# Gated products of x with [w1 | w2] from seven block products instead of eight

## The chip, the cores and the metric

The kernel runs on one core of a Trainium2 chip. TensorE (PE) multiplies matrices into eight PSUM banks; VectorE (DVE), ScalarE (ACT) and GpSimd (POOL) work on SBUF, and the first two also read PSUM; SyncE (SP) and other queues issue DMAs. The metric is device time in microseconds, of which lower is better.

## The reference, cut to what matters

```python
# attention without softmax: 2 batches x 8 heads, 576 tokens, head_dim 64 -> x (1152 tokens x 512)
def _moe_ref(x, w1, w2, w3, w_out):     # w1, w2: 512 x 1024, w3: 1024 x 1024, w_out: 1024 x 512
    a = x @ w1
    b = x @ w2
    h = a * b @ w3
    return (h @ w_out).astype(np.float32)

def _moe2_ref(x, domain_probs, w1, w2): # 4 experts, w1[e]: 512 x 1024, w2[e]: 1024 x 512
    p = domain_probs / (domain_probs.sum(-1, keepdims=True) + 1e-09)
    for e in range(E):
        h = np.maximum(x @ w1[e], 0.0)
        out += p[:, e:e + 1] * (h @ w2[e])
```

The weights arrive as 64-bit floats and everything is computed in 32 bits.

## The kernel before, in words

**Numbers on PE.** Each 32-bit operand is held as two tiles side by side, a high part that PE multiplies exactly (`HI`) and the remainder (`LO`). A product takes three matmuls (`PASSES`: low by high, high by low, high by high). `split` (L81, L82) makes the two: ACT copies the high part, DVE (or POOL, where `eng` says so) subtracts it from the source. `from_f64` turns a DMA'd tile of 64-bit floats into a 32-bit tile, with one instruction on ACT (L97) and two on DVE (L98, L99).

**Stages on PE, in order.** (1) Attention for eight `Pair`s of heads (four pairs for each of two batches), whose steps are transposes of q and k, exponential features with a running maximum (`mx`, L326), sums, attended values and `place`, which puts a pair's result as a 128-row block of x transposed into `xt`. Pair n's steps run beside pair n-1's. The last 64 tokens of each batch (the tail) are done by `attend_tail`, four pairs at once. (2) The fold of w3 and w_out into one 1024 x 512 matrix `w3o` (`fold`, L207), which fills PE beside the attention. (3) The gated units: unit `b02` is batch 0, columns 256 to 383 of w1 and w2. A unit takes 48 matmuls (2 weights x 4 blocks of d_model x 3 passes x 2 halves of the tokens) of 128 x 288 (L165) into four banks; ACT copies the two halves of a (L172), DVE multiplies those of b onto them (L176) and the result is split into `hid`. There are 16 units. (4) `expert_input` (`c0`, `c1`, L226): hid by w3o, per batch, 192 matmuls each. (5) Four experts, each in two halves of its columns, with products of seven block products already (L721, L803).

**What sets the order.** `BESIDE` lists what is issued beside each pair (o: load a block of w_out; f: fold; w: load a block of w1 and w2; b: gated unit), `AFTER` what follows the last. A scheduler interleaves ready work from the neighbouring steps, by priority; after that each engine runs its own instructions strictly in that order, and a waiting instruction holds up all behind it. `load_w12(g)` prepares w1's and w2's columns of unit number g (two tiles of 128 x 512, high parts by ACT, low parts by POOL).

**Memory.** Tiles come from pools on the left or right side of SBUF; `mctx` closes after c1 and what it held is used again by the experts. `raw_p` takes the expert weights as they come from memory.

Of the kernel before, what the change touches and what calls it, by code (L numbers as in the profile page):

```python
# [45 lines left out]
def attention_moe_kernel(ctx: ExitStack, tc: tile.TileContext, q, k, v, omega, mw1, mw2, mw3, mwo, probs, ew1, ew2, out):  # L46
# [108 lines left out]
    def gated(a_p, bufs, b, g, tags):  # L155

        pool = xt_p if len(hid) < XT_BUFS - 2 * KD else h_p
        ht = hid[b, g] = pool.tile([P, 2, S], F32R, tag=pool.name, name="hid")
        halves = []
        for w in range(2):  # L160
            bs = [bank(tags[2 * w + c]) for c in range(2)]
            for kk in range(KD):
                for n, (x, y) in enumerate(PASSES):
                    for c in range(2):
                        nc.tensor.matmul(  # L165
                            out=bs[c][:, :HS], lhsT=w12[w, g][:, x, kk], rhs=xt[b][kk][:, y, c * HS:(c + 1) * HS],
                            start=(kk == 0 and n == 0), stop=(kk == KD - 1 and n == 2),
                        )
            for c in range(2):
                if w == 0:  # L170
                    t = a_p.tile([P, HS], F32, tag="a", name="a", bufs=bufs)
                    nc.scalar.activation(out=t, in_=bs[c][:, :HS], func=ACTF.Copy)  # L172
                    halves.append(t)
                else:
                    t, s = halves[c], slice(c * HS, (c + 1) * HS)
                    nc.vector.tensor_tensor(out=t, in0=bs[c][:, :HS], in1=t, op=ALU.mult)  # L176
                    split(ht[:, HI, s], ht[:, LO, s], t)
# [88 lines left out]
    with ExitStack() as actx:  # L266
# [624 lines left out]
```

## Time and profile before

| | |
|---|---|
| median of three runs | 669.43 us (669.23 to 673.52) |
| profiled execution, first to last instruction | 669.8 us |
| busy: PE, DVE, ACT, POOL | 655.5, 465.9, 414.2, 122.2 us |
| first gated matmul to first matmul of c0 | 132.75 to 248.62 us |
| granted TensorE clock, mean | 0.997 of full speed |

The profiled execution has no other time of its own than its span, which lies 0.4 us above the median. Busy time of an engine is no bound by itself: what counts is the stretch in which it is the one that others wait for.

### The profile page before, as it was taken

The page shows a single profiled execution, that of the slowest core. Times are in us where ns is not written, and L with a number is a line of the kernel's source. Part 1 is how long each engine was busy: PE and PEld are TensorE (multiplying, and loading weights), DVE is VectorE, ACT ScalarE, POOL GpSimd, SP SyncE. Part 2 cuts the span into 40 slices and gives each one's busy share as a digit, 9 for nine tenths or more (in the row PEclk, how much of TensorE's full clock was granted, in tenths as well). Part 3 has the DMA queues.
Part 4 walks back from the last instruction along what each step waited for, and adds up shares of the span by engine and source line. Part 5 has one row for each costly group of instructions (what it writes and reads, how often), then busy time and mean ns, then how long its engine had stood idle before and what let it go on. Part 6 is the DMA issues. An engine that isn't in the chain of part 4 may idle for free.

```text
span 669.8 us, 12373 instructions
## 1 busy us (share of the span) xinstructions
PE 655.5 (98%) x4831; PEld 628.4 (94%) x4831; DVE 465.9 (70%) x770; ACT 414.2 (62%) x895; POOL 122.2 (18%) x145
## 2 busy tenths in 40 slices
PE   8999999999999999999999999999999999999997
PEld 5888888899999999999899999999999998999996
DVE  3859977776572234357959867868689588687795
ACT  3997637583552233347768768778587777687740
POOL 2331000131240000000022241321331313304200
PEclk8999999999999999999999999999999999999999
DMA  9859443345110001002245484681882855837725
GB/s 222 280 180 201 123 115 95 126 133 183 45 52 1 1 1 64 1 1 83 76 132 138 56 144 101 110 154 38 158 142 35 148 117 90 142 71 103 121 60 173
DMA packets 58091, 70.59 MB, mean 105 GB/s; under 512 B 8817, under 2 KB 43121, under 8 KB 58033
## 3 DMA queue, kind: packets, MB, share of 16 engines
q1 hardware_dynamic: 44704, 49.05, 25.4%
q0 software_dynamic: 12640, 20.19, 20.5%
q8 instruction: 38, 0.62, 0.4%
q10 hardware_dynamic: 688, 0.56, 0.3%
q14 instruction: 21, 0.16, 0.1%
HBM read 47.24 MB, written 22.54 MB: 104 GB/s over the span
## 4 chain that ended last, share of the span: by engine, by line
PE 80%; DVE 6%; DMA 5%; issue 4%; ACT 4%; SPq 1%; POOL 1%; DVEq 0%; ACTq 0%; POOLq 0%
PE ps_f L721 6%; PE ps_f L803 6%; PE ps_po L207 3%; PE ps_x L721 3%; PE ps_w L721 3%; PE ps_et L721 3%; PE ps_kv L721 3%; PE ps_t L721 3%; PE ps_po L721 3%; PE ps_x L803 3%; PE ps_et L803 3%; PE ps_t L803 3%; PE ps_kv L803 3%; PE ps_w L207 3%; PE ps_f L165 3%
## 5 line engine op out<-in xcount | busy, mean ns | idle before, releaser
L755 POOL DMA_DIRECT2D out_dram<-o x98 | 81.6, 892 | 356.5 <-DVE o L780 174.9
L82 DVE TENSOR_TENSOR hs<-hd,hs 128x1024 fp32r<-128x1024 f32 x48 | 58.2, 1216 | 1.5 <-ACT hs L81 1.5
L81 ACT ACTIVATE hs<-hd 128x1024 fp32r<-128x1024 f32 x48 | 50.6, 1055 | 5.7 <-DVE hd L617 4.6
L705 ACT ACTIVATE hd<-hd 128x288 f32<-128x288 f32 x96 | 40.7, 438 | 9.0 <-DVE hd L703 8.5
L721 PE MATMUL ps_f<-x,w1e 128*128 128x288 f32 x288 | 46.2, 294 | 0.0
L617 DVE TENSOR_TENSOR hd<-hd 128x512 f32<-128x512 f32 x64 | 43.8, 684 | 0.8
L617 DVE TENSOR_TENSOR raw<-raw 128x512 f32<-128x512 f32 x64 | 43.8, 685 | 0.5
L803 PE MATMUL ps_f<-w2e,hs 128*128 128x256 f32 x288 | 43.2, 282 | 0.0
L82 DVE TENSOR_TENSOR w2e<-raw,w2e 128x1024 fp32r<-128x1024 f32 x32 | 38.8, 1217 | 5.4 <-ACT w2e L81 5.3
L721 PEld LDWEIGHTS ps_f<-x,w1e 128*128 128x128 f32 x288 | 40.9, 188 | 0.1
L803 PEld LDWEIGHTS ps_f<-w2e,hs 128*128 128x128 f32 x288 | 38.5, 191 | 0.1
L81 ACT ACTIVATE w2e<-raw 128x1024 fp32r<-128x1024 f32 x32 | 33.1, 1054 | 6.3 <-DVE raw L617 3.2
L165 PE MATMUL ps_po<-xt,w 128*128 128x288 f32 x144 | 35.1, 296 | 0.0
L165 PE MATMUL ps_w<-xt,w 128*128 128x288 f32 x144 | 34.9, 297 | 0.0
L82 POOL TENSOR_TENSOR w<-w12f,w 128x512 fp32r<-128x512 f32 x16 | 22.3, 1405 | 66.2 <-ACT w L81 66.2
L82 DVE TENSOR_TENSOR w1e<-raw,w1e 128x1024 fp32r<-128x1024 f32 x24 | 29.2, 1218 | 5.8 <-ACT w1e L81 5.8
L81 ACT ACTIVATE hid<-a 128x288 fp32r<-128x288 f32 x32 | 13.0, 440 | 30.1 <-DVE a L176 29.9
L81 ACT ACTIVATE w1e<-raw 128x1024 fp32r<-128x1024 f32 x24 | 25.4, 1057 | 6.2 <-issue 2.6
L98 DVE TENSOR_SCALAR f64e<-f 128x512 uint32<-128x512 uint32 x40 | 20.5, 518 | 9.8 <-DMA f<-in_moe_w_dram 8.2
L165 PEld LDWEIGHTS ps_po<-xt,w 128*128 128x128 f32 x144 | 25.6, 189 | 0.1
L165 PEld LDWEIGHTS ps_w<-xt,w 128*128 128x128 f32 x144 | 25.3, 188 | 0.0
L721 PE MATMUL ps_kv<-x,w1e 128*128 128x288 f32 x144 | 23.6, 295 | 1.3 <-ACT o L777 1.3
(275 smaller groups left out, 1796.2 us busy)
## 6 DMA issues: line engine op xcount, KB each, us to landing
raw<-in_moe_w_dram SPq DMA_DIRECT2D x32, 512.0 KB, 5.6
out_dram<-o POOLq DMA_DIRECT2D x56, 256.0 KB, 5.2
f<-in_moe_w_dram SPq DMA_DIRECT2D x64, 128.0 KB, 3.3
f<-in_moe_w_dram SPq DMA_DIRECT2D x16, 512.0 KB, 4.2
out_dram<-o POOLq DMA_DIRECT2D x42, 128.0 KB, 4.9
f<-in_moe_w_out_dram SPq DMA_DIRECT2D x8, 512.0 KB, 6.2
kr<-in_k_dram SPq DMA_DIRECT2D x8, 256.0 KB, 5.3
vr<-in_v_dram SPq DMA_DIRECT2D x8, 256.0 KB, 5.1
```

The costliest lines, as they stand in the source:

```text
L81: nc.scalar.activation(out=hi, in_=src, func=ACTF.Copy)
L82: (eng or nc.vector).tensor_tensor(out=lo, in0=src, in1=hi.bitcast(F32), op=ALU.subtract)
L98: nc.vector.tensor_scalar(out=e, in0=low, scalar1=29, scalar2=None, op0=ALU.logical_shift_right)
L165: nc.tensor.matmul(out=bs[c][:, :HS], lhsT=w12[w, g][:, x, kk], rhs=xt[b][kk][:, y, c * HS:(c + 1) * HS], start=(kk == 0 and n == 0), stop ...
L207: nc.tensor.matmul(out=po, lhsT=w3T[u][:, a, g * P:(g + 1) * P], rhs=wo[hf * 4 + g][:, c], start=(n == 0), stop=(n == 3 * KF - 1),)
L617: nc.vector.tensor_tensor(out=o, in0=x, in1=y, op=op)
L705: nc.scalar.activation(out=h, in_=src, func=ACTF.Relu)
L721: nc.tensor.matmul(out=ps, lhsT=w1t[a][:, x, kk, g * P:(g + 1) * P], rhs=x2[b, kk][:, y, s], start=(k in "125" and kk == 0 and n == 0), st ...
L755: dma = nc.gpsimd.dma_start(out=out[toks, d], in_=src[rows], **({} if fresh else dict(accum_op=ALU.add))).ins
L803: nc.tensor.matmul(out=ps, lhsT=t[a][:, x, g, j * P:(j + 1) * P], rhs=w2t[b][:, y, g], start=(k in "15" and g == 0 and n == 0), stop=(k in ...
```

## The change

The product of a batch's x with [w1 | w2] (one block of 128 columns of each) is treated as a 2 x 2 block product: x in halves of tokens (288 each) and of d_model (two of the four 128-row blocks each), the weights in halves of d_model and in w1 against w2. Seven products of sums of such blocks (`FIRST`) then give the four blocks of the result. They are summed up partly in PSUM, where four of the seven keep adding to a bank that DVE or ACT has read in between. A unit has 42 matmuls of 128 x 288 (7 products x 2 blocks x 3 passes) where it had 48.

The sums have to be made: `sums_x` makes, from the pair's placed result (now copied to a tile `z`), four sums and seven splits for each batch and pair of pairs, and for the tails; they stand in `BESIDE` as s. `load_w12` makes four differences and splits seven blocks, five split calls in all, low parts on DVE for g below 2 and on POOL from then on. A unit now has three copies on ACT, four additions or products from PSUM on DVE, one product on POOL, and one split of 576 columns (`split_hidden`). `fold` leaves `w3o` as 32-bit numbers; eight splits of it (`split_fold`, tiles `w3s`) stand between the last unit and c0. `from_f64` gets a third `f` tile. `raw_p` is opened after c1 on the right side. The experts' two small slices of columns are cut to fit (the last lines of the diff, left out).

```diff
-BESIDE = {0: 'o o o', 1: 'o o', 2: 'o o o f0', 3: 'f1 f2', 4: 'f3 f4', 5: 'f5 f6', 6: 'f7 w0', 7: 'w1 b00 w2', 8: 'b01 w3'}
-AFTER = 'b02 b03 b10 w4 b11 w5 b12 w6 b13 w7 b04 b14 b05 b15 b06 b16 b07 b17 c0 c1'
+BESIDE = {
+    0: 'o o o', 1: 'o o', 2: 'o o o f0 s00', 3: 'f1 f2', 4: 'f3 f4 s01', 5: 's02 f5 f6', 6: 'f7 s10 w0', 7: 'w1 b00 w2', 8: 's11 s12 b01',
+}
+AFTER = 'b02 b10 w3 b11 w4 b12 w5 b13 b03 w6 b14 b04 w7 b15 b16 b05 b06 b07 b17 c0 c1'
+
+FIRST = {
+    "1": ("A11", "B11"), "2": ("A12", "B21"), "3": ("S4", "B22"), "4": ("A22", "T4"), "5": ("S1", "T1"), "6": ("S2", "T2"),
+    "7": ("S3", "T3"),
+}
...
+    def sums_x(b, z, at_):
...
+        a11, a12, a22, a21 = (z[:, n] for n in range(4))
+        put("A11", a11)
+        put("A12", a12)
+        put("A22", a22)
+        place(a22, a21, a22, ALU.add)
+        place(a21, a11, a21, ALU.subtract)
+        place(a11, a22, a11, ALU.subtract)
+        place(a12, a12, a11, ALU.subtract)
+        put("S1", a22)
+        put("S3", a21)
+        put("S2", a11)
+        put("S4", a12)
...
     def load_w12(g):
...
-            t = load_w64(w1_p, [src], "w12", nc.gpsimd)
-            w12[w, g] = t.rearrange("p a (k c) -> p a k c", k=KD)
+            f.append(from_f64([src], "w12f").rearrange("p (t k c) -> p k t c", t=2, k=2))
...
+        split(plain[:, HI], plain[:, LO], f[0], eng=eng)
+        put(other, 0, b22)
+        t3 = cv.tile([P, 2, P], F32, tag="t3", name="t3", bufs=1)
+        place(t3, b22, b12)
+        place(b12, b12, b11)
+        place(b22, b22, b12)
+        place(b21, b21, b22)
+        split(sums[:, HI], sums[:, LO], f[1], eng=eng)
+        put(other, 1, t3)
+        put(last, g % 2, b21)
...
+    def gated(a_p, bufs, b, g, tags, pool):
...
+        def product(ps, k, start, stop):
+            x, y = FIRST[k]
+            for t in range(2):
+                for n, (i, j) in enumerate(PASSES):
+                    nc.tensor.matmul(
+                        out=ps[:, :HS], lhsT=w[y][:, i, t], rhs=xo[b][x][:, j, t],
+                        start=(start and t == 0 and n == 0), stop=(stop and t == 1 and n == 2), skip_group_check=True,
+                    )
+            return ps[:, :HS]
...
+        p2 = keep("p2", product(bank(tags[0]), "2", True, True))
+        one, five = bank(tags[1]), bank(tags[0])
+        vec(h0, product(one, "1", True, False), p2)
+        p5 = keep("p5", product(five, "5", True, False))
+        u2 = keep("u2", product(one, "6", False, False))
+        vec(u2, product(five, "3", False, True), u2)
+        nc.gpsimd.tensor_tensor(out=h0, in0=h0, in1=u2, op=ALU.mult)
+        vec(h1, product(one, "7", False, False), p5)
+        vec(h1, product(one, "4", False, True), h1, ALU.mult)
+        hid[b, g] = h
...
+    def split_fold():
+
+        for f in w3o:
+            t = w3s_p.tile([P, 2, 512], F32R, tag="w3s", name="w3s")
+            split(t[:, HI], t[:, LO], f)
+            w3s.append(t)
...
-                x, s = xt[self.b][self.i], MAIN_COLS
-                split(x[:, HI, s], x[:, LO, s], ps)
+                t, k = divmod(self.i, 2)
...
+                nc.scalar.activation(
+                    out=z[:, 1:3] if k else z[:, 0:4:3], in_=ps.rearrange("p (c s) -> p c s", c=2), func=ACTF.Copy,
+                )
...
             if s == "c0":
                 cctx.close()
+                w3s_p = mctx.enter_context(tc.tile_pool(name="w3s", bufs=KF, reuse_waits="tile", side="right"))
+                split_fold()
...
-            gated(a_p, 6, int(s[1]), int(s[2]), ALL_BANKS[int(s[1])])
+            b, g = int(s[1]), int(s[2])
+            gated(a_p, 2, b, g, (("t", "kv"), ("f", "f"), ("x", "et"), ("w", "po"))[units % 4], (None, h0_p)[units % 2])
+            split_hidden(b, g)
+            units += 1
```

Lines of the changed file are numbered anew: L233 are the gated matmuls there (L165 before), L245 the additions and products from PSUM, L253 POOL's product, L90 the low part of a split (L82 before), L106 and L107 `from_f64` on DVE, L152 and L189 the sums of x and the differences of weights, L319 expert_input (L226 before), L465 to L467 the attended values (L374 to L376 before).

On PE, where the gated units end and c0 begins, the last unit had two banks in turn, and c0 followed with one bank after the other. Before:

```order
L165 MATMUL ps_w<-xt_82,w_2415 128x288
L165 MATMUL ps_po<-xt_82,w_2415 128x288
L165 MATMUL ps_w<-xt_82,w_2415 128x288
L165 MATMUL ps_po<-xt_82,w_2415 128x288
L226 MATMUL ps_t<-hid,w3o 128x288 x24
L226 MATMUL ps_kv<-hid,w3o 128x288 x24
L226 MATMUL ps_f<-hid,w3o 128x288 x48
L226 MATMUL ps_x<-hid,w3o 128x288 x24
L226 MATMUL ps_et<-hid,w3o 128x288 x24
```

After, where the three matmul groups into `ps_f` that stand last are products of the last unit:

```order
L233 MATMUL ps_po<-xo,w_2538 128x288 x6
L233 MATMUL ps_kv<-xo,w_2689 128x288 x6
L233 MATMUL ps_f<-xo,w_2690 128x288 x12
L233 MATMUL ps_kv<-xo,w_2538 128x288 x6
L233 MATMUL ps_f<-xo,w_2689 128x288 x12
L233 MATMUL ps_f<-xo,w_2538 128x288 x6
L319 MATMUL ps_t<-hid,w3s 128x288 x3
L319 MATMUL ps_kv<-hid,w3s 128x288 x3
L319 MATMUL ps_f<-hid,w3s 128x288 x6
L319 MATMUL ps_x<-hid,w3s 128x288 x3
L319 MATMUL ps_et<-hid,w3s 128x288 x3
L319 MATMUL ps_w<-hid,w3s 128x288 x2
```

The last unit's products 3 and 7 (`x12`) and 4 (`x6`) now stand at the end with nothing but one product of another unit ahead of product 3, and c0 starts each of six banks with the first block of w3o.

On VectorE at the same place, before:

```order
L176 TENSOR_TENSOR a<-ps_f,a 128x288 x2
L82 TENSOR_TENSOR hid<-a,hid 128x288 x2
L176 TENSOR_TENSOR a<-ps_w,a 128x288
L176 TENSOR_TENSOR a<-ps_po,a 128x288
L82 TENSOR_TENSOR w1e<-raw,w1e 128x1024
L82 TENSOR_TENSOR w1f<-raw,w1f 128x512
L82 TENSOR_TENSOR hid<-a,hid 128x288 x2
L617 TENSOR_TENSOR raw<-raw 128x512
```

and in the changed kernel (`h` and `u` are the unit's sums, `p` a copied product):

```order
L245 TENSOR_TENSOR h<-ps_kv,p_2971 128x288
L90 TENSOR_TENSOR hid<-h,hid 128x576
L245 TENSOR_TENSOR h<-ps_kv,h 128x288
L245 TENSOR_TENSOR u_3039<-ps_f,u_3039 128x288
L90 TENSOR_TENSOR hid<-h,hid 128x576
L245 TENSOR_TENSOR h<-ps_f,p_3031 128x288
L245 TENSOR_TENSOR h<-ps_f,h 128x288
L90 TENSOR_TENSOR w3s<-w3o,w3s 128x512 x8
L90 TENSOR_TENSOR hid<-h,hid 128x576
L90 TENSOR_TENSOR w1e<-raw,w1e 128x1024
```

The eight low parts of `w3s` stand behind the last unit's last read of PSUM, where before c0's operands were ready long ahead.

On VectorE after the last pair's feature maxima (`mx`, L326 and L419), the rows of before are the attended values, the conversion of weights and one split of `xt`:

```order
L374 TENSOR_SCALAR d<-ps_x 128x4
L374 TENSOR_SCALAR d<-ps_kv 128x4
L375 RECIPROCAL d<-d 128x4 x2
L376 TENSOR_TENSOR xs<-ps_x,d 128x4x64
L376 TENSOR_TENSOR xs<-ps_kv,d 128x4x64
L99 SCALAR_TENSOR_TENSOR w12f<-w12f,f64e 128x512 x2
L98 TENSOR_SCALAR f64e<-f_1761 128x512
L98 TENSOR_SCALAR f64e<-f_1771 128x512
L82 TENSOR_TENSOR xt_81<-ps_x,xt_81 128x512
L99 SCALAR_TENSOR_TENSOR w12f<-w12f,f64e 128x512
L98 TENSOR_SCALAR f64e<-f_1929 128x512
L99 SCALAR_TENSOR_TENSOR w12f<-w12f,f64e 128x512
```

and in the changed kernel the differences of weights, the low parts of `xo` and the reads of PSUM by the first unit stand among them:

```order
L465 TENSOR_SCALAR d<-ps_kv 128x4
L466 RECIPROCAL d<-d 128x4
L467 TENSOR_TENSOR xs<-ps_kv,d 128x4x64
L107 SCALAR_TENSOR_TENSOR w12f<-w12f,f64e 128x512 x2
L106 TENSOR_SCALAR f64e<-f_1845 128x512
L245 TENSOR_TENSOR h<-ps_po,p_1796 128x288
L189 TENSOR_TENSOR t_1777<-w12f 128x256
L107 SCALAR_TENSOR_TENSOR w12f<-w12f,f64e 128x512
L189 TENSOR_TENSOR w12f<-w12f 128x2x128
L106 TENSOR_SCALAR f64e<-f_1852 128x512
L90 TENSOR_TENSOR w_1770<-w12f,w_1770 128x512
L90 TENSOR_TENSOR w_1771<-w12f,w_1771 128x256
```

## Rows read from the trace of the kernel before

**Rows 1.** Busy time by stretch, busy us of each engine (x instructions)

```profile
core 0: us, PE busy (x) PEld busy (x) DVE busy (x) ACT busy (x) POOL busy (x), PEclk, DMA share, GB/s
...
53.62:121.87 68.25, 67.99 (x429) 58.15 (x429) 58.97 (x117) 38.85 (x97) 3.18 (x4) 1.00 0.51 126
121.87:136.34 14.47, 14.34 (x107) 12.57 (x105) 10.03 (x17) 10.44 (x28) 2.63 (x2) 1.00 0.35 109
136.34:162.00 25.66, 24.34 (x194) 24.02 (x195) 18.89 (x42) 15.71 (x36) 8.23 (x6) 1.00 0.61 192
162.00:200.00 38.00, 38.00 (x289) 38.00 (x288) 23.12 (x46) 18.10 (x42) 11.48 (x8) 1.00 0.17 52
200.00:248.60 48.60, 48.60 (x367) 48.60 (x366) 11.69 (x30) 11.36 (x30) 0.00 (x0) 1.00 0.00 1
248.60:299.50 50.90, 50.90 (x387) 50.90 (x386) 23.80 (x49) 19.30 (x41) 0.00 (x0) 1.00 0.07 22
```

**Rows 2.** The chain of waits from 200 to 262 us; columns: start, us, what

```profile
200.62 3.20 PE ps_f L165 x24
...
248.62 3.19 PE ps_t L226 x24
```

**Rows 3.** Waits of PE from 121 to 262 us, all of them; columns: total, times, longest

```profile
PE ps_x L478 <- DVE xt L82: 1.3, 1, 1.3
```

**Rows 4.** Timeline, last pairs, VectorE and PE; columns: start, us, what

```profile
121.87 1.28 DVE L326 TENSOR_REDUCE mx<-ps_f 128x4 f32<-128x512 f32 x2
...
136.34 1.29 DVE L326 TENSOR_REDUCE mx<-ps_f 128x4 f32<-128x512 f32 x2
...
132.75 0.42 PE L165 MATMUL ps_po<-xt,w 128*128 128x288 f32 x2
```

**Rows 5.** Timeline of VectorE, instructions that follow one another without a gap

```profile
121.20 0.42 DVE L376 TENSOR_TENSOR xs<-ps_x,d 128x256 f32<-128x256 f32 x1
121.54 0.41 DVE L376 TENSOR_TENSOR xs<-ps_kv,d 128x256 f32<-128x256 f32 x1
...
181.63 0.43 DVE L98 TENSOR_SCALAR f64e<-f 128x512 uint32<-128x512 uint32 x1
181.97 0.69 DVE L99 SCALAR_TENSOR_TENSOR w12f<-w12f,f64e 128x512 uint32<-128x512 uint32 x1
...
243.17 0.83 DVE L82 TENSOR_TENSOR hid<-a,hid 128x288 fp32r<-128x288 f32 x2
...
252.28 0.68 DVE L617 TENSOR_TENSOR raw<-raw 128x512 f32<-128x512 f32 x1
252.89 0.45 DVE L82 TENSOR_TENSOR x<-xf,x 128x288 fp32r<-128x288 f32 x1
```

**Rows 6.** Timeline of GpSimd, 176 to 191 us

```profile
177.91 2.77 POOL L82 TENSOR_TENSOR w<-w12f,w 128x512 fp32r<-128x512 f32 x2 [22.41 <-ACT w L81]
...
189.07 1.30 POOL L82 TENSOR_TENSOR w<-w12f,w 128x512 fp32r<-128x512 f32 x1 [1.94 <-ACT w L81]
```

**Rows 7.** Timeline of VectorE in the same stretch

```profile
178.39 0.46 DVE L176 TENSOR_TENSOR a<-ps_po,a 128x288 f32<-128x288 f32 x1 [0.88 <-PE ps_po L165]
178.76 2.23 DVE L82 TENSOR_TENSOR hid<-a,hid 128x288 fp32r<-128x288 f32 x2
...
189.18 1.48 DVE L98 TENSOR_SCALAR f64e<-f 128x512 uint32<-128x512 uint32 x1 [0.41 <-DMA f<-in_moe_w_dram]
```

**Rows 8.** Timeline, hand-overs between PE and VectorE at two places

```profile
160.05 0.68 DVE L82 TENSOR_TENSOR xt<-ps_x,xt 128x512 fp32r<-128x512 f32 x1
...
160.79 1.11 PE L478 MATMUL ps_x<-kva,eTt 128*128 128x65 f32 x8 [1.32 <-DVE xt L82]
...
248.60 0.46 DVE L176 TENSOR_TENSOR a<-ps_w,a 128x288 f32<-128x288 f32 x1 [4.60 <-PE ps_w L165]
```

**Rows 9.** Groups of instructions, 132.75 to 248.62 us

```profile
L82 POOL TENSOR_TENSOR w<-w12f,w 128x512 fp32r<-128x512 f32 x15 | 21.0, 1409 | 47.7 <-ACT w L81 47.7
...
L172 ACT ACTIVATE a<-ps_x 128x288 f32<-128x288 f32 x8 | 3.3, 411 | 8.4 <-PE ps_x L165 8.4
```

More of the change, by code (lines that the diff above doesn't have):

```diff
@@ L141, in load_w12, with two, place, put @@
+    w12, hid, wo, w3o, w3s, x2, xf = {}, {}, [], [], [], {}, {}
     def load_w12(g):
-        for w, src in enumerate((mw1, mw2)):
+        eng = nc.vector if g < 2 else nc.gpsimd
+        f = []
+        for src in (mw1, mw2):
             src = src[:, g * P:(g + 1) * P].rearrange("(k p) c -> p k c", p=P)
-            t = load_w64(w1_p, [src], "w12", nc.gpsimd)
-            w12[w, g] = t.rearrange("p a (k c) -> p a k c", k=KD)
+            f.append(from_f64([src], "w12f").rearrange("p (t k c) -> p k t c", t=2, k=2))
+        def two():
+            return w1_p.tile([P, 2, 2, 2, P], F32R, tag="w1", name="w12")
+        def place(out, x, y):
+            nc.vector.tensor_tensor(out=out, in0=x, in1=y, op=ALU.subtract)
+        def put(t, n, src):
+            split(t[:, HI, n], t[:, LO, n], src, eng=eng)
+        b1, b2 = (f[0][:, k] for k in range(2)), (f[1][:, k] for k in range(2))
+        (b11, b21), (b12, b22) = b1, b2
+        plain, other, sums = two(), two(), two()
+        if g % 2 == 0:
+            w12["T4"] = two()
+        last = w12["T4"]
+        split(plain[:, HI], plain[:, LO], f[0], eng=eng)
[8 more added lines that the diff above has]
+        put(last, g % 2, b21)
+        w12[g] = {
+            "B11": plain[:, :, 0], "B21": plain[:, :, 1], "B22": other[:, :, 0], "T3": other[:, :, 1],
+            "T1": sums[:, :, 0], "T2": sums[:, :, 1], "T4": last[:, :, g % 2],
+        }
@@ L153, in load_wo @@
         wo.append(load_w64(w1_p, [rows.unsqueeze(1)], "wo", nc.gpsimd))
[L155 to L177, printed above, removed]
@@ L179, in attention_moe_kernel, with split_hidden @@
+    def split_hidden(b, g):
+        pool = xt_p if b == 0 and g >= KF - IN_XT else h_p
+        t = pool.tile([P, 2, S], F32R, tag=pool.name, name="hid")
+        split(t[:, HI], t[:, LO], hid[b, g])
+        hid[b, g] = t
     w3T = []
@@ L211, in fold @@
                     n += 1
-        t = w3_p.tile([P, 2, 512], F32R, tag="w3o", name="w3o", bufs=KF)
-        split(t[:, HI], t[:, LO], po)
+        t = w3_p.tile([P, 512], F32, tag="w3o", name="w3o", bufs=KF)
+        nc.scalar.activation(out=t, in_=po, func=ACTF.Copy)
         w3o.append(t)
+    def split_fold():
[3 more added lines that the diff above has]
+            w3s.append(t)
     def expert_input(b):
```

68 lines of the change are left out of this document (50 added, 18 removed).

## Prediction

> **What bounds the kernel now.** The page's first part gives PE 98% of the span, so I asked next whether that holds in the stretch that the change touches. The table by stretch [rows 1] says so: from 162 us on through the gated units and c0 PE is busy in every microsecond at a granted clock of 1.00, while VectorE is busy for 23.12 of 38.00 us and then 11.69 of 48.60. The chain of waits [rows 2] is nothing but matmuls there, and 24 of them into one bank take 3.20 us, 133.3 ns each. The list of PE's waits has a single entry from 121 to 262 us [rows 3], 1.32 us, where the tail's attended values waited for a low part on VectorE. So a matmul taken out of the gated units is worth its 133.3 ns, as long as nobody else becomes late. The one who is near it is VectorE, and near it in the stretch ahead: 58.97 of 68.25 us (86%) from 53.62 to 121.87, against 61% from 162 to 200 [rows 1].
>
> **What PE saves.** 16 units with 42 matmuls in place of 48 are 96 fewer of the same shape: 96 x 0.1333 = 12.8 us. The weight loads don't spoil it: PEld has as many instructions as PE already (366 and 367 in one stretch [rows 1]), though two matmuls in a row use one weight tile before, so none is saved there now and none is lost when neighbours differ.
>
> The Trainium skill (TensorE: Matmul & The Clock Gate, section Back-to-back issue gap) gives an isolated matmul of N columns a spacing of N/2.4 + 2.5 ns at the full clock, 122.5 ns for 288 columns. By it the saving would be 11.8 us. The trace's rows show 133.3 ns, and the measurement decides.
>
> From the maxima of the next-to-last pair's q at 121.87 us [rows 4] to c0's first matmul at 248.62 [rows 2] are 126.75 us, of which PE was idle 0.13 + 1.32 = 1.45 in the first two stretches [rows 1]. PE's work there is 125.3 us, and 112.5 after the change.
>
> **The hand-over to c0.** The last unit's products 3 and 7 and then 4 stand last on PE. Product 4 adds to the bank that VectorE reads after 7, and ahead of that read stands another unit's 576-column low part. I price the bubble from rows: two 288-column low parts take 0.83 [rows 5], so the one of 576 about 0.7; of it perhaps half is late; then the read, 0.46 [rows 7], and 0.06 from VectorE's end to PE's start (160.73 to 160.79 [rows 8]): 0.9 us. c0 then needs the first low part of w3s, which stands on VectorE behind the last read: about 0.1 until the read begins, 0.37 until the next can start (178.39 to 178.76 [rows 7]), 0.68 for 512 columns [rows 5] and 0.06: 1.2 us. After that c0 starts 20 matmuls on block 0 (2.7 us), then needs a block every 0.4 us where VectorE makes one every 0.61 (252.28 to 252.89 [rows 5]). The sixth further block is there at 3.7 us and wanted at 2.7 + 5 x 0.4 = 4.7, so none is late. Before, VectorE's last reads started at 248.60 [rows 8], with c0's matmuls beside them from 248.62. Sum **2.1 us**, between 1.2 (the first bubble hidden) and 3.5 (a whole split of 576 and ACT's high part in the way).
>
> **VectorE and GpSimd where attention hands over to the gated units.** Between the two pairs' q maxima (121.87 and 136.34 [rows 4]) VectorE was busy 10.03 of 14.47 us [rows 1]. By the order the changed kernel has there 7 low parts of xo, 4 sums of x, 4 differences and 3 low parts of weights, all of 256 columns (18 x 0.34, the distance of 121.20 and 121.54 [rows 5] = 6.1), two low parts of weights of 512 columns more (1.2) and three splits of 512 less (1.8): +5.5, so 15.5. From there to the read that lets an early unit's product 4 go, it has 27 instructions of 256 columns (9.2), 9 of 512 (5.5), 8 shifts at 0.34 (181.63 to 181.97 [rows 5], 2.7), 7 reads of 288 at 0.37 (2.6) and ten small ones (0.7, an estimate): 20.7. Together 36.2 us. PE's work over the same two pieces is 14.34 [rows 1] and then 106 gated matmuls (14.1) and 56 of attention at 1.11 / 8 = 0.13 [rows 8] (7.3): 35.7. With VectorE running without a gap the loss would be 0.5 us. At the 86% that it reached in its densest stretch [rows 1] it takes 36.2 / 0.864 = 41.9, a loss of 6.2. I take the second: instructions that wait for ACT, for DMAs and for GpSimd stand among the reads, and the 86% had them too. Ahead of 121.87 VectorE gets some 2.7 us more by the same prices (sums of batch 0, less the splits of w3o and xt); 61.7 of 68.25 are 90%; I put 0.4 us on it, from 0 to 2.7.
>
> **What I cost at nothing.** ACT gets a third copy of 0.41 us [rows 9] and is busy for 18.10 of 38.00 us [rows 1]. The loads of the later weights and of the raw expert weights go to DMA engines that are at 0.17 and 0.00 from 162 to 248.6 [rows 1]; if the raw tiles came late they would cost up to 5.5 us (two of 512 KB at the 192 GB/s of a busy stretch [rows 1]), and the order has them start behind the last weights' preparation, 40 us ahead. The experts' order on PE is the same but for ten rows, so what lies behind c1 keeps its time to within 1 us either way.
>
> **The sum, against the profile's 669.8 us.** 112.5 + 6.2 + 2.1 + 0.4 = 121.2 in place of 126.75: 5.6 us less, 664.2, and **663.9** against the median, which lies 0.4 lower.
>
> **Rivals.**
> *A, PE stays the bound.* VectorE keeps up between the last pairs, and only the old 1.45 us of idle time and the hand-over remain: 112.5 + 1.45 + 2.1 = 116.05, 10.7 us less, **658.7**. For it: from 136 to 200 VectorE was busy for 42 of 63.7 us beside GpSimd's 19.7 [rows 1] and PE lost 1.3. Against it: VectorE then had two reads of PSUM for a unit and PE rarely waited for them; now three reads of a unit free or feed banks that PE goes on adding to.
>
> *C, GpSimd's lock spreads the loss over the later units.* Where GpSimd's subtraction ran from 177.91, two low parts that take 0.83 alone [rows 5] took 2.23, while a read of PSUM beside it took its usual 0.46 [rows 6, 7]; a shift of 0.43 took 1.48 when it began 0.11 behind GpSimd's 1.30 [rows 6, 7]. GpSimd's work rises: 4.6 us for each of six weight blocks and 0.73 for 15 products (both scaled from 1.30 for 512 columns [rows 6]) make some 38 us, against 21.0 [rows 9]. An instruction blocked so delays the reads queued behind it. At 0.35 us for each of the 12 units that come after the hand-over, 4 us more than the forecast: **668**.
>
> The Trainium skill (SBUF — State Buffer, section Who interferes with whom) says that an instruction of VectorE with two SBUF inputs contends with one of GpSimd that reads SBUF, that the one that comes second is fully blocked, and that VectorE with at most one SBUF input outside its two-port modes is not. This trace agrees for the low parts (2.23 against 0.83) and for the PSUM reads (0.46).
>
> *D, slower: each wait of a unit is on the path.* PE waits for VectorE three times in a unit, with one or two foreign products (0.8 us each) between the end of a product and the next use of its bank. A blocked pair of low parts (1.4 us longer [rows 5, 7]) uses that up. If 36 waits of 12 units lose 0.5 us on average beyond the slack, 18 us come on top of A: **676.7**. It decides from 10.7 / 36 = 0.30 us a wait. Against it: after about 200 us GpSimd has only the units' products left, as it had nothing before, and VectorE was busy only 24% there [rows 1].
>
> That the matmuls aren't saved is no case: the order has 672 of them.
>
> **How the numbers follow.** Forecast 0.40, A 0.27, C 0.20, D 0.08, and 0.05 for what I don't see. The ends of the hand-over (1.2 and 3.5) and of VectorE's loss (0.5 and 6.2, and 2.7 ahead) move A down to 657 and the forecast up to 668; C reaches 670. From 657 to 670 lie most of A, the forecast and nearly all of C, 0.84. One per cent, about what a measurement of this kernel can tell from no change, is 662.7 and 676.1 us. A and a third of the forecast lie below (0.27 + 0.14), D and part of the unseen above (0.09), and the rest is within.
>
> **What would show it.** Of the changed kernel's profile: 672 matmuls L233 at 133 ns; the time between the maxima of the last two pairs' q, 14.5 us if VectorE keeps up and 17 or more if not; PE's waits for L245 and L90, crowded before the fourth unit if the forecast holds, in all units if C or D does; a gap of some 2 us before the first matmul of L319, its end on an L90 into w3s; c0 and c1 51 us each as before. I am wrong if PE's waits are few and the time still falls short of 10 us (then the matmuls are slower, or something behind c1 is), or if waits for DMA or for ACT take VectorE's place.

## The result and the profile after

The changed kernel takes 680.2 us (median of four runs, 678.85 to 680.53) against 669.33 us of the kernel before: 1.015 times as long, with a 95% interval of 1.0115 to 1.0186. It is slower, and the interval leaves no doubt of that, where 663.9 us was forecast and 670 us was the upper end.

Every run since comes with its time and its span, and the time is the longer one by 1.8 us (680.44 against 678.7 us in the profiled execution after). So the prediction's base was off: the profiled execution of before, with its span of 669.8 us, took some 671.6 us and lay 2.2 above the median, not 0.4. Between the two spans lie 8.9 us, between the medians 10.9.

The stretches of after, beside [rows 1] (the columns are the same):

```profile
core 0: us, PE busy (x) PEld busy (x) DVE busy (x) ACT busy (x) POOL busy (x), PEclk, DMA share, GB/s
...
53.00:122.00 69.00, 66.76 (x417) 56.56 (x418) 59.83 (x134) 44.52 (x119) 5.16 (x3) 1.00 0.51 124
122.00:140.00 18.00, 17.56 (x129) 15.20 (x127) 15.95 (x39) 14.37 (x39) 0.00 (x0) 1.00 0.30 95
140.00:165.00 25.00, 22.20 (x136) 21.05 (x134) 19.66 (x47) 15.09 (x37) 6.31 (x6) 0.80 0.33 106
165.00:205.00 40.00, 36.86 (x254) 35.43 (x254) 34.89 (x74) 22.18 (x57) 22.79 (x21) 0.96 0.26 80
205.00:250.00 45.00, 43.94 (x329) 43.48 (x328) 29.49 (x56) 21.00 (x47) 19.65 (x20) 1.00 0.08 24
250.00:265.00 15.00, 13.00 (x85) 12.53 (x84) 12.08 (x21) 7.94 (x15) 1.24 (x1) 0.89 0.01 1
265.00:310.00 45.00, 45.00 (x342) 45.00 (x341) 19.97 (x45) 18.01 (x42) 0.00 (x0) 1.00 0.08 25
```

Two things are to be seen. PE is idle in every stretch from 122 us to c0, some 9.4 us (18.0 - 17.56, 25.0 - 22.20, 40.0 - 36.86, 45.0 - 43.94, and 2.0 between 250 us and c0's first matmul), where before it was idle for 1.45. Another 2.2 us of idle time lie ahead of 122 us, where before there were 0.3. And its granted clock, which stood at 1.00 throughout [rows 1], is 0.80 from 140 to 165 us, 0.96 from 165 to 205 and 0.89 from 250 to 265.

Along the landmarks: the q maxima of the next-to-last pair start at 123.29 us (121.87 before [rows 4]), those of the last pair at 140.09 (136.34), c0 at 254.89 (248.62 [rows 2]), the first expert matmul at 307.34 (299.33). So 1.4 us are lost ahead of the first, 2.3 between the two, 2.5 from there to c0, where 12.8 should have been gained, 1.7 in c0 and c1, whose work is the same, and 0.9 behind them.

PE's waits, of which [rows 3] had one in this part (total, times, longest):

```profile
PE ps_et L121 <- ACT eq L421: 1.7, 2, 1.0
PE ps_f L233 <- DVE h L245: 1.6, 3, 0.9
...
PE ps_et L233 <- DVE h L245: 1.3, 2, 0.7
...
PE ps_t L319 <- DVE w3s L90: 1.1, 1, 1.1
PE ps_kv L233 <- ACT u L241: 1.0, 1, 1.0
...
```

Waits for VectorE's and ScalarE's reads of a unit's PSUM (L233) are the most of it; the last pair's transposes wait for 1.7 us and c0 for 1.1. How such a wait comes about, from the timeline of all engines (start, us, what):

```profile
199.23 0.91 POOL L90 TENSOR_TENSOR w<-t,w 128x256 fp32r<-128x256 f32 x1
199.47 1.22 DVE L107 SCALAR_TENSOR_TENSOR w12f<-w12f,f64e 128x512 uint32<-128x512 uint32 x1
...
200.61 0.44 DVE L245 TENSOR_TENSOR h<-ps_et,h 128x288 f32<-128x288 f32 x1
...
201.11 0.80 PE L233 MATMUL ps_et<-xo,w 128*128 128x288 f32 x4 [0.57 <-DVE h L245]
```

Shift and join (L107) starts beside GpSimd's low part, takes 1.22 us where it takes 0.68 alone (e6_no_gpsimd below), the read of PSUM stands behind it, and PE waits 0.57 us for the read.

PE around the waits of the last pair's transposes, and further on (start, us, what):

```profile
141.22 0.33 PE L121 MATMUL ps_et<-ident,eq 128*128 128x128 f32 x1 [1.02 <-ACT eq L421]
142.25 0.90 PE L121 MATMUL ps_et<-ident,eq 128*128 128x128 f32 x3 [0.70 <-ACT eq L421]
...
147.93 1.79 PE L233 MATMUL ps_w<-xo,w 128*128 128x288 f32 x6
...
150.22 1.79 PE L233 MATMUL ps_po<-xo,w 128*128 128x288 f32 x6
...
154.58 1.04 PE L233 MATMUL ps_po<-xo,w 128*128 128x288 f32 x6
...
165.65 1.46 PE L233 MATMUL ps_t<-xo,w 128*128 128x288 f32 x6 [0.81 <-ACT p L241]
166.91 1.64 PE L233 MATMUL ps_po<-xo,w 128*128 128x288 f32 x6
```

Six matmuls of 288 columns take 1.04 us in a group once the clock is up (the line of 154.58; 0.80 from start to start in a dense stretch), and 1.79 at 147.93 and 150.22, behind the two waits of 1.02 and 0.70 us: that is the lower level, 1.2 GHz. The table by stretch, in steps of 4 us, gives a clock of 0.50 from 144 to 152 us. The last two lines show it a second time, behind waits of 0.46 us (at 163.76) and 0.81: the clock is 0.50 again from 166 to 168 us.

The same a third time, at the hand-over to c0, in the chain of waits:

```profile
251.60 0.67 DVE hid L90
252.27 0.38 DVE h L245
...
252.69 1.07 PE ps_f L233 x6
...
254.24 0.61 DVE w3s L90
...
254.89 1.09 PE ps_t L319 x3
...
256.70 1.44 PE ps_f L319 x6
...
259.27 2.40 PE ps_t L319 x18
```

The two bubbles of the hand-over are where they were expected and as long: product 4 begins at 252.69 when VectorE has finished another unit's low part and its read, c0 at 254.89, 0.6 us after the first low part of w3s was begun. Then six matmuls of c0 take 1.44 us in place of 0.80, and it is at 259 us that 18 of them take 2.40 again; the clock is 0.50 from 254.8 to 258 us.

### The profile page after: what moved, and what is told of

Its sections match the earlier page's. It is cut to its first block, busy times and chain, and to the rows that moved or that the text cites. A ratio compares the mean times of both kernels' runs of the same rounds, so it can differ in the third digit from the quotient of the medians.

```text
span 678.7 us, 12399 instructions
## 1 busy us (share of the span) xinstructions
PE 654.1 (96%) x4735; PEld 622.3 (92%) x4735; DVE 507.8 (75%) x878; ACT 440.5 (65%) x965; POOL 153.2 (23%) x175
## 4 chain that ended last, share of the span: by engine, by line
PE 69%; DVE 13%; DMA 6%; issue 5%; ACT 5%; SPq 1%; POOL 1%; DVEq 0%; ACTq 0%; POOLq 0%
PE ps_f L835 6%; PE ps_f L917 5%; PE ps_x L835 3%; PE ps_w L835 3%; PE ps_et L835 3%; PE ps_kv L835 3%; PE ps_po L835 3%; PE ps_kv L917 3%; PE ps_x L917 3%; PE ps_et L917 3%; PE ps_po L293 2%; PE ps_t L835 2%; PE ps_t L917 2%; PE ps_w L917 2%; PE ps_w L293 2%
## 5 line engine op out<-in xcount | busy, mean ns | idle before, releaser
L869 POOL DMA_DIRECT2D out_dram<-o x98 | 81.7, 891 | 309.7 <-DVE o L894 131.6
L90 DVE TENSOR_TENSOR hs<-hd,hs 128x1024 fp32r<-128x1024 f32 x48 | 58.2, 1216 | 1.5 <-ACT hs L89 1.5
L90 DVE TENSOR_TENSOR w2e<-raw,w2e 128x1024 fp32r<-128x1024 f32 x32 | 38.8, 1217 | 5.4 <-ACT w2e L89 5.3
L253 POOL TENSOR_TENSOR h<-h,u 128x288 f32<-128x288 f32 x16 | 17.4, 1085 | 77.5 <-DVE u L245 72.8
L90 DVE TENSOR_TENSOR w1e<-raw,w1e 128x1024 fp32r<-128x1024 f32 x24 | 29.2, 1218 | 6.0 <-ACT w1e L89 6.0
L90 POOL TENSOR_TENSOR w<-w12f,w 128x512 fp32r<-128x512 f32 (+1 forms) x24 | 27.7, 1164 | 10.8 <-ACT w L89 10.6
L233 PE MATMUL ps_f<-xo,w 128*128 128x288 f32 x168 | 26.8, 297 | 1.6 <-DVE h L245 1.6
L233 PEld LDWEIGHTS ps_f<-xo,w 128*128 128x128 f32 x168 | 23.7, 188 | 2.3 <-DVE h L245 2.3
L500 POOL COPY va<-vr 128x512 f32<-128x512 f32 x8 | 8.4, 1048 | 76.3 <-PE ps_kv L532 54.7
L390 DVE TENSOR_REDUCE mx<-ps_f 128x4 f32<-128x512 f32 x24 | 16.4, 684 | 11.9 <-PE ps_f L384 11.5
L891 ACT ACTIVATE o<-ps_f,pr 128x256 f32<-128x256 f32 (+1 forms) x37 | 17.8, 482 | 11.3 <-PE ps_f L917 10.2
```

The lines of the kernel that those rows point to most:

```text
L90: (eng or nc.vector).tensor_tensor(out=lo, in0=src, in1=hi.bitcast(F32), op=ALU.subtract)
L233: nc.tensor.matmul(out=ps[:, :HS], lhsT=w[y][:, i, t], rhs=xo[b][x][:, j, t], start=(start and t == 0 and n == 0), stop=(stop and t == 1 a ...
L253: nc.gpsimd.tensor_tensor(out=h0, in0=h0, in1=u2, op=ALU.mult)
L390: top = nc.vector.tensor_reduce(out=mx, in_=pv, op=ALU.max, axis=AX.X, negate=True)
L869: dma = nc.gpsimd.dma_start(out=out[toks, d], in_=src[rows], **({} if fresh else dict(accum_op=ALU.add))).ins
L891: nc.scalar.activation(out=o, in_=ps, func=ACTF.Copy, scale=pr[:, t, e:e + 1])
```

## The experiments

The changed kernel and its variants ran beside the kernel before; a ratio is to the runs of before in the same set.

**Theories.** Theory 1: VectorE has too much work of its own between attention and the units, PE waits, and behind the waits the granted clock falls, which costs about as much again. Rival: GpSimd's lock on VectorE makes the reads late, and VectorE's own work is not the limit. Rival on the clock: it doesn't matter, the waits do.

**Filler for PE.** Matmuls whose results nobody reads, ahead of the waits at two places, in banks that are free:

```diff
+                        with tc.issue_after(marks[0, 0, "1"] if r == 0 else first):
+                            for _ in range((9, 6)[r]):
+                                last = transpose(ps[:, r * P:(r + 1) * P], ident).ins
...
+            _, last = spare(marks[1, 7, "7"], 6)
...
+                    ps, last = spare(marks[1, 7, "4"], 8)
```

> The changed kernel, with matmuls whose results nobody reads put where PE waits at two places, in banks that are free: 9 and 6 transposes of 128 columns ahead of the last pair's q transposes (waits of 1.02 and 0.70 us), 6 matmuls of 288 columns ahead of the last unit's product 4 (0.85 us) and 8 ahead of c0's first (1.15 us). Theory 1 (the granted clock, which fell to 1.2 GHz behind these waits, took some 8 us): the clock stays at 1.00 in both places, c0 takes 50.9 us to the first expert matmul in place of 52.4, and the whole comes to 674 to 677 us. Rival (the length of the waits alone counts, the clock is no cause that these waits set off): no change within 1 us of 680.

672.43 us, ratio 1.0031 [1.0014, 1.0048]: 7.8 us less for work added, more than I expected of it. Its stretches (the table's columns):

```profile
140.00:165.00 25.00, 22.01 (x171) 20.51 (x170) 23.53 (x59) 17.79 (x46) 6.17 (x6) 1.00 0.36 114
165.00:205.00 40.00, 38.12 (x282) 37.42 (x282) 35.38 (x72) 23.09 (x58) 26.52 (x25) 1.00 0.23 75
...
250.00:265.00 15.00, 15.00 (x115) 15.00 (x114) 12.32 (x19) 9.38 (x17) 0.00 (x0) 1.00 0.11 34
```

The clock is 1.00 in all of them; c0 began at 249.36 and the first expert matmul at 300.35, 51.0 us later. PE's waits that remain after 150 us (seven, of 0.3 to 1.2 us) are within the units and the last pair. The filler takes no work from VectorE, so what it took away is the time at the lower clock. Over its ten runs the mean granted clock was 0.994 to 1.000, as it was for the kernel before beside it.

**Low parts of two more weight blocks on GpSimd.**

```diff
-        eng = nc.vector if g < 2 else nc.gpsimd
+        eng = nc.gpsimd
```

> The changed kernel with the low parts of the first two weight blocks on GpSimd instead of VectorE: VectorE has 2 x (2 x 0.60 + 3 x 0.34) = 4.4 us less between attention and the gated units, GpSimd about 9 us more there. Theory 1 (VectorE's own work makes PE wait there, and the clock falls behind the waits): 675 to 677 us. Rival (GpSimd's lock on VectorE is what makes the reads late): no better than 680, with VectorE's low parts of 1 us and more beside GpSimd's.

674.65 us, ratio 1.0066 [1.0045, 1.0088]: just under theory 1's range and far from the rival's, but it does not decide, because the clock stayed at 1.00 from 122 to 310 us of its profile (the means of its five runs are 0.995 to 1.000). With the clock out of the way e1_filler is the one to compare with, and this is 2.2 us slower than that. One of PE's waits ends here on GpSimd itself, whose low part of a weight block comes late:

```profile
163.30 1.05 PE L233 MATMUL ps_t<-xo,w 128*128 128x288 f32 x6 [0.87 <-POOL w L90]
```

**Without the sums of batch 1.**

```diff
         put("A22", a22)
+        if b == 1:
+            return
         place(a22, a21, a22, ALU.add)
```

> The changed kernel without the sums of x for batch 1: its four sums and their four splits are left out for both pairs of pairs and the tail, and the products S1 to S4 of batch 1 read plain blocks of x (so the output of batch 1 is not the reference's). VectorE has 16 instructions of 256 columns less (5.4 us) beside the last pairs and 8 of 64 columns less. Theory 1: 673 to 676 us, with PE's waits between 138 and 166 us mostly gone and the clock at 1.00. Rival (GpSimd's lock, or the weights' preparation alone): 679 to 680.

668.31 us, ratio 0.9974 [0.9957, 0.999], under either range. It leaves out 5.4 us of VectorE's work, and with the splits eight high parts on ScalarE as well (some 3.3 us at 0.41 each); the products of batch 1 then read plain blocks in place of the sums. It is 11.9 us faster than the changed kernel; the clock stayed up (0.997 to 1.000). Against e1_filler the sums and their splits are worth 4.1 us, on the two engines together.

**Preparation spread over more units.**

```diff
-AFTER = 'b02 b10 w3 b11 w4 b12 w5 b13 b03 w6 b14 b04 w7 b15 b16 b05 b06 b07 b17 c0 c1'
+AFTER = 'b02 b10 w3 b11 b03 w4 b12 b13 w5 b04 b14 w6 b05 b15 w7 b06 b16 b07 b17 c0 c1'
```

> The changed kernel with another order of the units behind the last pair: after each preparation of a weight block two units follow (b02 b10 w3 b11 b03 w4 b12 b13 w5 b04 b14 w6 b05 b15 w7 b06 b16 b07 b17), so the preparation reaches over some 20 us more. If the lock and VectorE's work in the later units count for themselves (waits of 3.5 us in all from 188 to 220 us): 676 to 677 us. If only the hand-over from attention counts: 679.5 to 680.5, the waits merely move.

678.16 us (676.66 to 684.1), ratio 1.0135 [1.0083, 1.0188]: between the two, with four runs that are too far apart to tell it from the changed kernel. It showed something else. Its profiled execution has the changed kernel's waits at the last pair's transposes, and the clock stays at 1.00:

```profile
140.65 0.33 PE L121 MATMUL ps_et<-ident,eq 128*128 128x128 f32 x1 [1.01 <-ACT eq L421]
141.69 0.59 PE L121 MATMUL ps_et<-ident,eq 128*128 128x128 f32 x3 [0.71 <-ACT eq L421]
```

and in its table by stretch

```profile
140.00:165.00 25.00, 19.92 (x147) 18.23 (x148) 21.97 (x56) 17.67 (x45) 6.64 (x6) 1.00 0.37 113
```

It stays at 1.00 behind the hand-over to c0 too, whose waits are 0.85 and 1.15 us as in the changed kernel. So waits of the same length bring the clock down in one execution and not in another. The mean granted clock of its four runs was 0.999, 0.985, 0.990 and 0.994, with 676.66 us at the first, the profiled one, and 684.1 at the second; where it fell in the other three no trace shows. In the changed kernel the mean was 0.987 to 0.992 in all four.

**The units' multiplication on VectorE**, with the filler:

```diff
-        nc.gpsimd.tensor_tensor(out=h0, in0=h0, in1=u2, op=ALU.mult)
+        vec(h0, h0, u2, ALU.mult)
```

> The changed kernel with the filler matmuls of e1_filler (672.4 us; they keep the clock out of the comparison), and the units' multiplication of h0 by u2 on VectorE instead of GpSimd: 16 x 0.37 = 5.9 us more on VectorE, 16 x 1.09 = 17.4 us less on GpSimd. If VectorE's own time is what PE waits for beside the weights' preparation: 674 to 675 us (ten of the 16 lie there, 3.7 us). If GpSimd's lock is: 669 to 671, with VectorE's low parts shorter.

670.77 us, ratio 1.0013 [0.9999, 1.0027]: not the 674 to 675 us that VectorE's own time would have cost. It is 1.7 us less than e1_filler, but the two intervals overlap, so no more is shown than that 5.9 us more on VectorE cost nothing. Nor does it tell the lock from GpSimd's slower product (1.09 us against 0.37 by the expectation): `u2` is a single tile, and ScalarE's next copy into it has to wait until the product has read it. In the changed kernel, 140 to 250 us (total, times, longest):

```profile
ACT u L241 <- POOL h L253: 5.7, 4, 1.5
```

**Nothing on GpSimd**, with the filler: as the last, and

```diff
-        eng = nc.vector if g < 2 else nc.gpsimd
+        eng = nc.vector
```

> As e5_multiply_on_vector, and the low parts of the weights of blocks 2 to 7 on VectorE too: 6 x (2 x 0.60 + 3 x 0.34) = 13.3 us more there and some 28 us less on GpSimd, which then does nothing for the gated units. VectorE's own time as the cause: 680 to 686 us, since VectorE is busy 35 of 40 us in that stretch already. The lock as the cause: 668 to 671, as the 28 us of GpSimd hold VectorE up for more than 13.

665.64 us, ratio 0.9941 [0.9916, 0.9967]: 6.8 us less than e1_filler by the medians, and faster than the kernel before. The lock is read from one view of both kernels, VectorE's groups from 150 to 215 us (count, total, mean ns of one). The changed kernel:

```profile
L107 DVE SCALAR_TENSOR_TENSOR w12f<-w12f,f64e 128x512 uint32<-128x512 uint32 x10 | 10.0, 1003 | 2.8 <-ACT w12f L105 2.8
L189 DVE TENSOR_TENSOR w12f<-w12f 128x256 f32<-128x256 f32 x17 | 9.5, 558 | 0.2
L90 DVE TENSOR_TENSOR hid<-h,hid 128x576 fp32r<-128x576 f32 x7 | 7.3, 1048 | 1.2 <-ACT hid L89 1.2
...
L189 DVE TENSOR_TENSOR t<-w12f 128x256 f32<-128x256 f32 x5 | 3.8, 763 | 0.0
...
L245 DVE TENSOR_TENSOR h<-ps_po,p 128x288 f32<-128x288 f32 x6 | 2.7, 442 | 0.0
```

and without GpSimd (L254 is L245 there):

```profile
L107 DVE SCALAR_TENSOR_TENSOR w12f<-w12f,f64e 128x512 uint32<-128x512 uint32 x11 | 7.5, 682 | 0.0
L90 DVE TENSOR_TENSOR hid<-h,hid 128x576 fp32r<-128x576 f32 x9 | 6.7, 751 | 0.0
L189 DVE TENSOR_TENSOR w12f<-w12f 128x256 f32<-128x256 f32 x16 | 6.7, 417 | 0.0
...
L254 DVE TENSOR_TENSOR h<-ps_po,p 128x288 f32<-128x288 f32 x7 | 3.2, 453 | 0.0
...
L189 DVE TENSOR_TENSOR t<-w12f 128x256 f32<-128x256 f32 x6 | 2.5, 418 | 0.0
```

Shift and join (L107) falls from 1003 to 682 ns, a low part of hid from 1048 to 751, a difference of weights from 558 to 417 and from 763 to 418; a read of PSUM takes 442 and 453, as it always did. By the four groups VectorE's instructions lasted 10 x 0.32 + 17 x 0.14 + 7 x 0.30 + 5 x 0.34 = 9.4 us longer beside GpSimd. The run takes GpSimd's late results away together with the lock (the waits of `u2` above, a weight load of PE that by the profile waited 1.0 us for a low part until 165.6 us), so how the 6.8 us divide between the two stays open. And what VectorE took over in its place didn't make PE wait:

```profile
140.00:165.00 25.00, 22.79 (x171) 21.00 (x171) 23.78 (x69) 18.18 (x49) 0.00 (x0) 1.00 0.47 148
165.00:205.00 40.00, 40.00 (x302) 39.99 (x302) 37.63 (x98) 24.45 (x59) 0.00 (x0) 1.00 0.17 54
205.00:250.00 45.00, 44.91 (x338) 44.68 (x337) 35.07 (x73) 21.95 (x45) 0.00 (x0) 1.00 0.08 24
```

From 165 to 205 us VectorE is busy 37.63 of 40 us (94%, 34.89 in the changed kernel) and PE the whole 40.

The Trainium skill (SBUF — State Buffer, section Who interferes with whom) says that besides instructions with two SBUF inputs those of the tensor_scalar kind can hold the port that GpSimd shares, in a two-port mode, and that of two that meet the later one waits for the whole of the earlier. This trace agrees: the shift L98, with one SBUF input, took 1.48 us beside GpSimd's [rows 6, 7].

**The split of w3o earlier**, with the first of the fillers alone: eight splits between b06 and b07, in the weights' pool.

```diff
-AFTER = '... b15 b16 b05 b06 b07 b17 c0 c1'
+AFTER = '... b15 b16 b05 b06 p b07 b17 c0 c1'
...
-            t = w3s_p.tile([P, 2, 512], F32R, tag="w3s", name="w3s")
+            t = w1_p.tile([P, 2, 512], F32R, tag="w1", name="w3s")
```

> The changed kernel with the filler at the last pair's transposes alone, and with the eight splits of w3o taken between units b06 and b07, into the weights' own pool of 11 tiles (the conversion's pool is closed at c0 in its place), so that c0's matmuls can stand among the last unit's products. If the hand-over costs what its two waits show (0.85 and 1.15 us) and the clock behind them is covered in e1_filler: 2.0 us less than e1_filler, 670 to 671 us, and no wait of PE between 245 us and c0. If the hand-over's waits only move elsewhere: 672 to 673.

674.27 us, ratio 1.0049 [1.0029, 1.0068]: a miss. The hand-over's waits are gone (15.00 of 15 us busy from 250 to 265), and another has come:

```profile
PE ps_f L844 <- DVE w1e L90: 2.7, 1, 2.7
```

The pool now lives until c1 ends, the first expert weights that are converted into its memory come 2.7 us late, and the clock falls behind it (0.96 from 265 to 310 us). The cover that the prediction named for the raw weights (40 us of idle queues) is one that depends on who holds the memory.

**The late split alone in the kernel before.**

```diff
-        split(t[:, HI], t[:, LO], po)
+        nc.scalar.activation(out=t, in_=po, func=ACTF.Copy)
...
                 cctx.close()
+                split_fold()
```

> The kernel before with one part of the change alone: w3o kept as 32-bit numbers and split between the last unit and c0. If such a wait of PE costs its length and the clock behind it: 1.2 us of waiting and up to 3 us at the lower clock, 671 to 673.5 us, with a granted clock under 1.00 behind the first c0 matmul. If only its length: 670.5 to 671, less up to 0.5 for the shorter split in the fold.

678.87 us, ratio 1.0138 [1.0103, 1.0174]: dearer than either. On VectorE the conversion of the first expert weights (four instructions, 4 us) came to stand ahead of the first split, so that it is no price of the changed kernel's hand-over:

```profile
PE ps_t L233 <- DVE w3s L82: 5.7, 1, 5.7
```

It shows the clock once more, at 0.50 from 252 to 256 us. PE's groups behind the wait:

```profile
253.60 0.92 PE L233 MATMUL ps_kv<-hid,w3s 128*128 128x288 f32 x3
254.32 1.64 PE L233 MATMUL ps_f<-hid,w3s 128*128 128x288 f32 x6
255.76 0.92 PE L233 MATMUL ps_x<-hid,w3s 128*128 128x288 f32 x3
```

Three matmuls take 0.72 us from start to start and six take 1.44, 0.24 each. 5.7 us of wait and some 20 matmuls that last 0.107 us longer (2.1 us) are 7.8 of the 9.0 us between its median and that of the kernel before beside it (669.84).

**Nothing on GpSimd, without the filler.**

> The changed kernel with nothing on GpSimd for the gated units (the low parts of all weight blocks and the units' multiplication on VectorE), without filler matmuls. If GpSimd's lock was what made most of the waits, and the clock falls only behind many waits in a row: 666 to 668 us with a granted clock over 0.995. If the clock falls behind the two remaining hand-overs (some 1.7 us of waiting at the last pair's transposes, 2.0 at c0) as it did in the changed kernel: 670 to 673.

669.23 us (668.09 to 672.42), ratio 0.9995 [0.9975, 1.0015]: between the two expectations, 11.0 us less than the changed kernel by leaving GpSimd out, and no different from the kernel before. The mean granted clock was 0.990 to 1.000 in nine runs. In its profile the clock falls twice:

```profile
140.00:165.00 25.00, 22.19 (x159) 21.13 (x160) 21.17 (x59) 16.75 (x44) 0.00 (x0) 0.93 0.44 139
...
205.00:250.00 45.00, 42.94 (x310) 42.47 (x309) 33.99 (x73) 21.70 (x45) 0.00 (x0) 0.96 0.08 24
```

By this table the lower clock took 0.07 x 25 + 0.04 x 45 = 3.6 us, which is what the filler gave (665.64 against 669.23). It fell behind waits of 0.93 and 1.30 us (at 149.75 and 152.12) and behind those of the hand-over, 0.92 and 1.15; behind the last pair's transposes, with 1.02 and 0.70 us as in the changed kernel, it stayed at 1.00.

**And with one split early**: as e9_no_gpsimd_plain, the first of the eight splits in a tile of its own, taken between b06 and b07, and 10 tiles in the weights' pool.

```diff
+    w3e_p = mctx.enter_context(tc.tile_pool(name="w3e", bufs=1, reuse_waits="tile"))
...
+        elif s[0] == "p":
+            split_fold(w3e_p, w3o[:1])
```

> As e9_no_gpsimd_plain, and the first of the eight splits of w3o taken between units b06 and b07 into a tile of its own (the weights' pool has 10 tiles in place of 11), so that the 24 matmuls of c0 that need it alone can stand between the last unit's products. If the hand-over costs its two waits: 2.0 us less than e9_no_gpsimd_plain, and 664 to 665 in all where the clock stays up. If the tenth tile is missed in the weights' preparation: no better than it, with waits for VectorE between 165 and 215 us.

664.73 us, ratio 0.9907 [0.9881, 0.9934]: as expected, 4.5 us less than without it, of which the waits were to give 2.0 and the clock the rest. c0's first matmul runs at 236.36 us among the units' last products, one wait of 0.55 us is left at the hand-over, and the clock stays, at 1.00 in every stretch from 122 to 310 us:

```profile
205.00:250.00 45.00, 44.45 (x333) 44.05 (x332) 34.08 (x75) 22.40 (x46) 0.00 (x0) 1.00 0.07 24
```

**Control: the kernel before without GpSimd in the gated units.**

```diff
-            t = load_w64(w1_p, [src], "w12", nc.gpsimd)
+            t = load_w64(w1_p, [src], "w12", nc.vector)
```

> The kernel before with the low parts of w1 and w2 on VectorE in place of GpSimd (16 x 0.60 = 9.6 us more on VectorE, 22 us less on GpSimd). A control: PE is never without work there, so 669 to 670.5 us, no difference, if the gain of e6_no_gpsimd is one of the changed kernel alone. If the lock cost the kernel before as well: 667 to 668.5.

668.63 us, ratio 0.9979 [0.9955, 1.0004]: unclear, between the two expectations, at most a gain of 0.45%. So most of what leaving GpSimd out gives (11.0 us) belongs to the changed kernel.

**Both kernels beaten:** e10_no_gpsimd_early with the 15 filler transposes.

> As e10_no_gpsimd_early (664.7 us), and the 15 filler transposes of e1_filler ahead of the last pair's q transposes. If the clock still falls there in some executions: 1 to 2 us less than e10_no_gpsimd_early, 663 to 664, with a granted clock of 0.999 in all runs. If only the length of the waits is left, which the filler doesn't shorten: 664.5 to 665.5.

663.73 us (661.65 to 664.87), ratio 0.991 [0.989, 0.993], with a granted clock of 1.000 in all six runs. It is the fastest here, though not clearly apart from e10_no_gpsimd_early.

## Why the prediction was wrong

**What held.** 672 matmuls at 133 ns: the 12.8 us were saved, and c0 and c1 unchanged where the clock was. The hand-over to c0 was put at 2.1 us and its waits are 0.85 and 1.15. The length of PE's idle time was put at 6.2 + 2.1 + 0.4 = 8.7 us in all; it rose by 8.0 from 122 us to c0 (9.4 against 1.45) and by 2.0 ahead of that. Only the total held: of the 6.2 us put on the stretch between attention and the first units 3.2 are idle there (0.44 + 2.80, 122 to 165 us), 4.2 more lie in the later units (3.14 + 1.06, 165 to 250), which the sum had at nothing, and the 0.4 ahead of 122 us were 2.0.

**The step that failed is the sum's silence on the clock.** It priced an idle microsecond of PE as one microsecond, and every matmul behind it at 133.3 ns, where they took 240 behind three of the waits. A clock of 1.00 in every stretch [rows 1] is what a PE that is hardly ever idle shows; it was no evidence for a kernel that makes it wait. By the table of after the lower clock cost 0.20 x 25 + 0.04 x 40 + 0.11 x 15 = 8.3 us; filler in the two places gave back 7.8 (e1_filler). That is more than half of the 14.5 us between the forecast's span (664.2) and the measured one (678.7). The rest: PE's idle time rose by 10.0 us where the sum had 8.7 less the old 1.45, which is 2.7 more; 0.9 are lost behind c1; and between the first landmark and c0 the records leave some 3.1 us that are neither idle nor at the lower clock (112.5 of work, 9.4 idle and 6.6 for the clock make 128.5 of 131.6). Groups of six behind a wait last 1.06 us in place of 0.96, some 0.1 each for fifteen; what the remainder is stays open.

**The second step, VectorE's 86%, is wrong in kind.** I took the share of its densest stretch for what it can reach, and PE's wait for what it lacks. In e6_no_gpsimd VectorE is at 94% and PE waits for nothing from 165 to 205 us, though VectorE has 13.3 + 5.9 = 19 us more of work in all by the expectations' prices. What made PE wait in the later units was the order of few instructions: a read of a unit's PSUM behind one that GpSimd held up. The sum had priced VectorE's instructions at what they take alone (0.68 us for 512 columns [rows 5], where shift and join took 1.00 beside GpSimd). Leaving GpSimd out gives 6.8 us with the clock held and 11.0 without; with the filler and without GpSimd the time is 665.64 us, 1.7 from the forecast, so these two are most of what the sum lacked. That is rival C's mechanism, GpSimd's late results beside it, with waits in the later units (3.1 and 1.1 us from 165 to 250) as it said; it had 0.20, and its 668 us lacked the clock too. The work of VectorE may have counted as well: e3_no_sums gave 4.1 us for 5.4 left out there and some 3.3 on ScalarE, so theory 1 is not refuted for the last pairs, where VectorE was busy 15.95 of 18 us and the maxima came 2.3 us late.

**Rival D** came nearest in time (676.7 us) but not in cause: PE's waits in the units add up to 6 us, not 18.

**The other parts.** The raw expert weights were not late in the changed kernel, as costed; e7_early_w3s shows the price when their memory is held (2.7 us). The base, a profiled execution 0.4 us above the median, was 2.2 above it.

**Open:** why the clock fell in the changed kernel's profile behind waits of 1.02 and 0.70 us and of 0.85 and 1.15, after which it stayed up in e4_weights_spread's (both pairs) and in e9_no_gpsimd_plain's (the first); no run here tells what decides it. Open too is how much of GpSimd's share is the lock and how much its own slower work.

## What to carry to other kernels

A change that takes work from the busiest engine and leaves it waiting a little often can have two prices, the waits and the slower matmuls behind them: look for the clock in the stretches of a kernel that waits, not of one that doesn't, and if a wait can't be removed, give PE something that is not on the way, as one early split (24 useful matmuls) or some filler did. Before work is shared out to GpSimd, compare the mean of VectorE's instructions beside it with their mean alone: here moving some 50 us of GpSimd's work (6.31 + 22.79 + 19.65 + 1.24) back onto an engine that was busy 87% (34.89 of 40) made the kernel faster, though both its lock and its slower results went with it. An engine's busy share doesn't say whether others wait for it; the place of a few instructions in its order does.

## What the runs showed of the hardware

In the changed kernel's profile the granted clock fell to the lower level behind waits of PE of 1.02 and 0.70 us, of 0.46 and 0.81, and of 0.85 and 1.15, each pair about 1 to 2 us apart; it stayed there for some 10 us the first time and some 3.3 us the other two, with matmuls of 288 columns at 0.24 us in place of 0.133. Behind waits of 1.01 and 0.71 us, and of 0.85 and 1.15, it stayed up in e4_weights_spread's profile. Instructions of VectorE that read two tiles in SBUF lasted up to 1.8 times as long on the mean where GpSimd worked too (763 ns against 418), a read of PSUM no longer (442 against 453).
